# Efficient attention followed by an MLP with exact GELU: order of the VectorE work between two chunks, kv scaled by ScalarE, v cast later

## The chip, the cores and the metric

The kernel runs on one core of a Trainium2 chip. The metric is the device time of one execution in microseconds (us). PE is the matrix engine, PEld its weight loads, DVE is VectorE, ACT is ScalarE, POOL is GpSimd, and SP issues most of the DMAs.

## The reference

```
B, H, S, D = 8, 8, 576, 64
q_s = exp(q) / sum over D            # softmax of each row of q
k_s = exp(k) / sum over S            # softmax of k along the sequence
kv  = einsum('bhsd,bhse->bhde', k_s, v)
att = einsum('bhsd,bhde->bhse', q_s, kv)
x   = att.transpose(0, 2, 1, 3).reshape(4608, 512)
h   = x @ w_in                       # 512 -> 2048
g   = 0.5 * h * (1 + erf(h / sqrt(2)))
out = g @ w_out                      # 2048 -> 512, fp32
```

(The reference subtracts the maximum before each exponential and adds 1e-09 to each sum.)

## The kernel before, in words

**Tiling.** The 4608 rows are worked in nine chunks c = 0 to 8. Chunk c < 8 is the first 512 rows of batch c; chunk 8 gathers the last 64 rows of the eight batches. All matrix work is in bf16 with fp32 sums in PSUM, whose eight banks of 128 x 512 fp32 are handed out by role names (`bb`, `ba`, `x0` to `x3`, `kv0`, `kv1`), and `turn_roles` permutes the roles after every chunk's hidden layer.

**Two phases per chunk.** From chunk 2 on, a chunk is `h_waves(c)`, the hidden layer with its GELU, and then `y_phase(c, ...)` (for chunk 8 `y_last`), the output layer. Both multiply 2 x 2 blocks with seven products in place of eight (Winograd's form of Strassen's scheme): PE issues seven products, and DVE and ACT form sums and differences before and after them.

In `h_waves` the products are `mm(m, q...)` for m = 1 to 7 and four column groups q. Each group has an accumulator of kind A (product 1, later 6, 7 and 4), one of kind B (5, later 3) and one of kind C (a `seed` copy of A, later 2). Products 5, 6, 7 and 4 read `t1`, `t2`, `t3`, `t4`, four differences of blocks of the transposed chunk `xT`, which `x_sums(c, (i,))` makes on DVE into the tile `quad_t` (512 columns of bf16 each). The start of `h_waves` for c > 2 is, in program order: `mm(1, 0, 1)`, `seed(0)` (ACT), `mm(5, 0, 1)`, `seed(1)` (ACT), two `p5_copy` (ACT, B into the SBUF tile `r`), `mm(6, 0, 1)`, `x_sums(c, (3,))`, `e_sum(0)` and `e_sum(1)` (DVE: A + r into B), `x_sums(c, (4,))`, `mm(2, 0, 1)`, GELU of C, `mm(7, 0, 1)`, and so on. `mm(7, q)` writes the accumulator that `e_sum(q)` reads, and so comes after it.

In `y_phase` for c > 2 the output block is built in two SBUF tiles `y_sb` of four parts c11, c12, c21, c22. Product 3 of the outer scheme is itself done by seven small products (class `Two`, results in the banks called `yf` and `yd`), which `t3.add` adds to c12 on DVE in pieces: "a", "b" and "c" come from `yd`, "e" and "d" from `yf`. The bank of `yd` has the role `kv1`, the bank of `yf` has the role `bb`. Product 4, `mm(4, pa, False)`, writes the bank `pa` after the DVE addition `tt(c22, halves(pa), c22)` has read it; ACT then copies `pa` to c21.

**Work for later chunks.** Between the small products and `mm(4)`, `next_x(c, nb, fn)` runs with nb = c + 2. It issues the matmuls of the next chunk's x (`x_all`) and copies them out of PSUM as `xT` (three copies by ACT, the second by DVE). It also issues the DMA transpose of q for chunk nb (`xbar_step`) and, while nb < 8, the kv product of batch nb (`kv_mm`, into the roles `kv0` and `kv1`) with its normalisation `kv_norm` on DVE. `x_sums(c + 1, (1,))` and `(2,)` stand around the additions "e" and "d" (argument `fn`) and `kv_norm`. For c = 6 and 7 there is no kv product.

POOL scales the exponentials of q for chunk nb (`q_scale_parts`, eight instructions), makes sums for `Two`, and casts v of batch nb to bf16 (`cast_v_all`, four instructions of line 190). The order on every engine is the order of the program.

Of the kernel before, what the change touches and what calls it, by code (L numbers as in the profile page):

```python
# [16 lines left out]
def kernel(  # L17
# [11 lines left out]
    nc = tc.nc  # L29
# [221 lines left out]
    def kv_step(b, mid=None):  # L251
# [3 lines left out]
            mid()  # L255
        kv_norm(b)

    def q_sums(b, i=0, n=1):

        w = H // n  # L260
        qsum = small.tile([128, J, w], FP32, tag="qsum")
        st[b]["recq"] = small.tile([128, J, w], FP32, tag="recq", name="recq")
        nc.vector.reduce_sum(out=qsum, in_=st[b]["eq"][:, :, i * w:(i + 1) * w, :], axis=AX.X)  # L263
        nc.vector.reciprocal(st[b]["recq"], qsum)  # L264
# [164 lines left out]
    def tt(out, in0, in1, op=ALU.add, eng=nc.vector):  # L429
        eng.tensor_tensor(out=out, in0=in0, in1=in1, op=op)  # L430
# [27 lines left out]
    def turn_roles():  # L458

        r = dict(roles)  # L460
        roles.update(bb=r["x3"], ba=r["kv1"], x0=r["bb"], x1=r["kv0"], x2=r["x0"], x3=r["ba"],
                     kv0=r["x1"], kv1=r["x2"])

    def h_waves(c, mid):


        h_begin(c)
        g, xT = st[c]["g"], st[c]["xT"]
        t1, t2, t3, t4 = (quad["t"][:, i] for i in range(4))
        mov = {1: xT[:, 0:2, 0:HT], 2: xT[:, 2:4, 0:HT], 3: xT[:, 2:4, HT:M], 4: t4, 5: t1, 6: t2, 7: t3}  # L470
        plain_w = {1: (0, 0), 2: (2, 0), 4: (2, HK)}
        sum_w = {3: 3, 5: 0, 6: 1, 7: 2}
        lo, hi = slice(0, HT), slice(HT, M)
        bank_of = {
            "A": ("x0", "bb", "x3", "ba"), "B": ("kv0", "kv1", "x1", "x2"), "C": ("x1", "x2", "kv0", "kv1"),
        }
        if mid:
            bank_of.update(B=("kv0", "kv1") * 2, C=("x1", "x2") * 2)
        held = {}

        def take(kind, q):
            held[kind, q] = bank(roles[bank_of[kind][q]], "q" + kind.lower(), (128, 2, HT))

        def mm(m, *qs):
            for q in qs:
                kind = {5: "B", 3: "B", 2: "C"}.get(m, "A")
                if m in (1, 5):
                    take(kind, q)
                for u in range(2):
                    for k in range(2):  # L490
                        if m in plain_w:
                            k0, t0 = plain_w[m]
                            t = 2 * q + t0 + u
                            w = wi_bf[:, k0 + k, t * 128:(t + 1) * 128]
                        else:
                            t = 2 * (q % 2) + u
                            w = quad["s"][q // 2][:, sum_w[m], k, t * 128:(t + 1) * 128]
                        nc.tensor.matmul(  # L498
                            held[kind, q][:, u], w, mov[m][:, k],
                            start=(m in (1, 5) and u == 0 and k == 0), stop=(k == 1),  # L500
                            skip_group_check=True,
                        )

        def seed(q, eng=nc.scalar.copy):
            take("C", q)
            eng(out=held["C", q], in_=held["A", q])

        def p5_copy(q, eng):
            held["r", q] = quad["r"][:, q]
            eng(out=held["r", q], in_=held["B", q])  # L510

        def e_sum(q):
            tt(held["B", q], held["A", q], held["r", q])

        def r_sum(q):
            tt(held["r", q], held["A", q], held["r", q])

        def gelu(kind, *qs):
            up, half = {"C": (1, lo), "B": (1, hi), "A": (0, lo), "r": (0, hi)}[kind]
            for q in qs:  # L520
                t = 2 * q + (0 if up else HK)
                nc.scalar.activation(out=g[:, t:t + 2, half], in_=held[kind, q], func=AF.Gelu)  # L522

        vcopy, scopy = nc.vector.tensor_copy, nc.scalar.copy
        mm(1, 0, 1)
        seed(0)
        if mid:
            seed(1)
            mm(1, 2, 3)
            mm(2, 0, 1)  # L530
            gelu("C", 0, 1)
            mm(5, 0, 1)
            p5_copy(0, scopy)
            p5_copy(1, scopy)
            x_sums(c, (3, 4))
            seed(2, vcopy)
            seed(3, vcopy)
            mm(6, 0, 1)
            e_sum(0)
            e_sum(1)  # L540
            mid()
            mm(2, 2, 3)
            gelu("C", 2, 3)
            mm(7, 0, 1)
            r_sum(0)
            r_sum(1)
            mm(3, 0, 1)
            gelu("B", 0, 1)
            mm(6, 2)
            mm(5, 2, 3)  # L550
            p5_copy(2, scopy)
            p5_copy(3, scopy)
            mm(6, 3)
            e_sum(2)
            e_sum(3)
            gelu("r", 0, 1)
            mm(4, 0, 1)
            gelu("A", 0, 1)
            mm(7, 2, 3)
            r_sum(2)  # L560
            r_sum(3)
            s_parts(c, 0, 4, (1,))
            gelu("r", 2, 3)
            mm(3, 2, 3)
            mm(4, 2, 3)
        else:
            mm(5, 0, 1)
            seed(1)
            p5_copy(0, scopy)
            p5_copy(1, scopy)  # L570
            mm(6, 0, 1)
            x_sums(c, (3,))
            e_sum(0)
            e_sum(1)
            x_sums(c, (4,))
            mm(2, 0, 1)
            gelu("C", 0, 1)
            mm(7, 0, 1)
            r_sum(0)
            r_sum(1)  # L580
            mm(3, 0, 1)
            for q in (2, 3):
                mm(5, q)
                mm(1, q)
            mm(4, 0, 1)
            gelu("r", 0)
            gelu("B", 0, 1)
            gelu("r", 1)
            seed(2)
            seed(3)  # L590
            gelu("A", 0, 1)
            p5_copy(2, vcopy)
            p5_copy(3, vcopy)
            s_parts(c, 0, 4, (1,))
            mm(6, 2, 3)
            e_sum(2)
            e_sum(3)
            s_parts(c, 0, 4, (2,))
            mm(2, 2, 3)
            gelu("C", 2, 3)  # L600
            mm(7, 2, 3)
            r_sum(2)
            r_sum(3)
            gelu("r", 2, 3)
            mm(3, 2, 3)
            mm(4, 2, 3)
        gelu("B", 2, 3)
        gelu("A", 2, 3)
        if mid:
            s_parts(c, 0, 4, (2, 3))  # L610
            s_parts(c, 4, 4, (1,))
            s_parts(c, 0, 4, (4,))
            s_parts(c, 4, 4, (2, 3, 4))
        else:
            s_parts(c, 0, 4, (3, 4))
            s_parts(c, 4, 4, (1, 2, 3, 4))
        turn_roles()
        if mid:
            roles.update(ba=roles["x2"], x2=roles["ba"])
# [133 lines left out]
    def y_phase(c, ins):  # L753
# [8 lines left out]
        def halves(ps):  # L762
            return ps.rearrange("p (j n) -> p j n", j=2)
# [34 lines left out]
        if t3:  # L798
            t3.mm(6, 5, 2, 4, 3)
            t3.add("b", c12)  # L800
            t3.mm(7)
            t3.add("c", c12)
        tt(c22, halves(pa), c22)
        after(7)
        if not t3:
            mm(3, pb, False)
# [337 lines left out]

        nc.gpsimd.tensor_copy(out=scr[:, 2:3], in_=s12[:, HK - 1, HT:HT + 1])

    def next_x(c, nb, fn=lambda: None):
        x_all(c + 1, [roles[n] for n in ("x0", "x1", "x2", "x3")], "svsv" if c == 2 else "svss")
        if nb <= B:
            xbar_step(nb)  # L1150

        def first():
            x_sums(c + 1, (1,))
            fn()

        if nb < B:
            kv_tiles(nb, (roles["kv0"], roles["kv1"]))
            kv_step(nb, first)
        else:
            first()  # L1160
        x_sums(c + 1, (2,))

    for c in range(2, B + 1):
        nb = c + 2
        if 2 < c < B - 2:
            cast_v_all(nb)
        h_waves(c, q_late if c == 2 else None)
        yi = {}
        if nb <= B:
            yi[1] = [lambda: exp_q(nb)]  # L1170
            yi[6] = [lambda: q_sums(nb), lambda: q_scale_parts(nb)]
            yi[7] = [lambda: table(AF.Gelu)]
        if nb + 1 < B:
            yi[6].append(lambda: load(nb + 1))
        elif nb + 1 == B:
            yi[6].append(load_qrest)
        if nb < B:
            yi[5] = [lambda: exp_k(nb), touch_s]
            if c == 2:
                yi[5].append(lambda: cast_v_all(nb))  # L1180
        if 2 < c < B:
            yi.setdefault(5, []).append(lambda: two[3].sums(c))
        if c < B:
            yi[3] = [lambda *fn: next_x(c, nb, *fn)]
            y_phase(c, yi)
        else:
            y_last(c)
# [30 lines left out]
```

## Time and profile before

| what | value |
|---|---|
| median of 3 runs | 258.31 us (257.98 to 258.41) |
| the profiled execution | 258.36 us, of which the span from the first to the last instruction is 256.5 us |
| granted TensorE clock | 1.00 |
| PE, PEld busy | 247.9 us (97%), 195.7 us (76%) |
| DVE, ACT, POOL busy | 198.7, 189.5, 82.1 us |
| PE's share of the chain that ended last | 87% |
| DVE's share of it | 6% |

Times in the trace count from the first instruction. A line of the timeline gives the start, the length from the first start to the last end of the merged instructions, the engine, the line of the kernel, the operation, output <- inputs, the shape and the count, and in brackets the idle time before it with what ended it. Instructions on one engine overlap a little at their ends, so the distance between two starts is shorter than the length of one.

### The profile page before, as it was taken

Reading aid. Unit: us, or ns where it says so; the run is one execution under the profiler, and the core shown is the slowest. Engines: PE = TensorE matmul, PEld = TensorE weight load, DVE = VectorE, ACT = ScalarE, POOL = GpSimd, SP = SyncE. Lnnn points to the kernel's source line nnn. Section 1 sums busy time; section 2 is a strip of 40 time slices with the busy share of each in tenths; the row PEclk is TensorE's granted clock in tenths of the full one; section 3 lists DMA queues with packets and bytes.
Section 4 is the critical chain, followed back from the end, with each engine's and each line's share of the span. In section 5 each row is a group of like instructions: output and inputs, shape, how many; then the busy total and the mean of one; then the engine's idle time right before and its main releaser. Section 6 shows DMA issues by size and latency. Waiting matters only on the chain.

```text
span 256.5 us, 6691 instructions
## 1 busy us (share of the span) xinstructions
PE 247.9 (97%) x2738; PEld 195.7 (76%) x2738; DVE 198.7 (77%) x358; ACT 189.5 (74%) x322; POOL 82.1 (32%) x109
## 2 busy tenths in 40 slices
PE   7799999999999999999999999999999899999994
PEld 3344444448888888888788978898889788988883
DVE  1878699878986977897989798987898689468932
ACT  4785988699887986898689868896886687068810
POOL 1530023001945078008900890086007600700000
PEclk9999999999999999999999999999999999999999
DMA  7999999993379998970389029201600160021033
GB/s 237 396 389 422 404 406 400 398 413 146 72 253 379 223 387 265 321 284 0 85 286 394 19 63 284 67 1 42 209 1 3 31 217 0 3 93 73 1 80 86
DMA packets 43166, 50.23 MB, mean 196 GB/s; under 512 B 20224, under 2 KB 30464, under 8 KB 42880
## 3 DMA queue, kind: packets, MB, share of 16 engines
q1 hardware_dynamic: 42416, 49.13, 55.8%
q10 hardware_dynamic: 720, 0.69, 1.1%
q8 instruction: 21, 0.34, 0.5%
q14 instruction: 9, 0.07, 0.1%
HBM read 36.70 MB, written 9.44 MB: 180 GB/s over the span
## 4 chain that ended last, share of the span: by engine, by line
PE 87%; DVE 6%; DMA 4%; issue 1%; ACT 0%; ACTq 0%; POOL 0%; DVEq 0%
PE qa L498 19%; PE ya L768 17%; PE ps L387 11%; PE qb L498 9%; PE yb L768 6%; PE ps L641 5%; PE qc L498 5%; PE yc L768 5%; DVE y_sb L430 3%; PE ya L837 2%; DMA f<-in_v_dram 2%; DMA touch<-in_moe_w_in_dram 2%; PE yf L726 2%; DVE quad_t L430 2%; PE yb L837 1%; PE yd L726 1%
## 5 line engine op out<-in xcount | busy, mean ns | idle before, releaser
L768 PEld LDWEIGHTS <-g 128*128 128x128 bf16 x448 | 43.1, 98 | 6.8 <-issue 1.4
L498 PEld LDWEIGHTS <-quad_s 128*128 128x128 bf16 x448 | 43.4, 98 | 6.2 <-DVE quad_t L430 0.9
L498 PEld LDWEIGHTS <-wi_bf 128*128 128x128 bf16 x336 | 32.9, 98 | 4.7 <-issue 0.8
L498 PE MATMUL qa<-quad_t,quad_s 128*128 128x256 bf16 x224 | 29.2, 273 | 0.3 <-DVE quad_t L430 0.2
L387 PE MATMUL ps<-xT,wi_bf 128*128 128x512 bf16 x128 | 28.1, 379 | 0.0
L768 PE MATMUL ya<-w,g 128*128 128x256 bf16 x224 | 26.8, 273 | 1.0 <-DVE y_sb L430 1.0
L768 PEld LDWEIGHTS <-s 128*128 128x128 bf16 x256 | 25.0, 98 | 2.9
L430 DVE TENSOR_TENSOR qb<-qa,r 128x512 f32<-128x512 f32 x28 | 18.2, 694 | 9.7 <-PE qa L498 5.1
L278 POOL TENSOR_TENSOR e<-e,recq 128x256 bf16<-128x256 bf16 x40 | 24.0, 637 | 4.6 <-issue 2.7
L269 POOL TENSOR_TENSOR e<-e,recq 128x1024 bf16<-128x1024 bf16 (+1 forms) x4 | 9.3, 2332 | 48.5 <-DVE recq L264 41.8
L380 ACT CAST xT<-ps 128x512 bf16<-128x512 f32 x23 | 12.3, 593 | 16.7 <-PE ps L358 8.4
L263 DVE TENSOR_REDUCE qsum<-e 128x16 f32<-128x1024 bf16 (+1 forms) x12 | 20.9, 1742 | 4.8 <-ACT e L173 4.8
L387 PEld LDWEIGHTS <-wi_bf 128*128 128x128 bf16 x128 | 12.4, 98 | 15.2 <-issue 0.5
L393 ACT ACTIVATE g<-ps 128x512 bf16<-128x512 f32 x32 | 17.6, 602 | 6.1 <-PE ps L387 5.8
L173 ACT ACTIVATE e<-f 128x512 bf16<-128x512 f32 (+1 forms) x42 | 20.5, 556 | 1.9 <-DMA f<-in_q_dram 1.7
L522 ACT ACTIVATE g<-r 128x512 bf16<-128x512 f32 x28 | 17.3, 631 | 5.8 <-DVE r L430 5.8
L430 POOL TENSOR_TENSOR two<-s 128x512 bf16<-128x512 bf16 x10 | 11.6, 1157 | 31.1 <-DVE s L430 31.1
L522 ACT ACTIVATE g<-qc 128x512 bf16<-128x512 f32 x28 | 15.3, 594 | 8.4 <-PE qc L498 8.3
L190 POOL CAST v_aug<-f 128x576 bf16<-128x576 f32 x25 | 18.0, 756 | 4.1 <-DMA f<-in_v_dram 3.1
L430 DVE TENSOR_TENSOR r<-qa,r 128x512 f32<-128x512 f32 x28 | 18.0, 684 | 1.0 <-PE qa L498 0.7
L178 ACT ACTIVATE ek<-f 128x2304 bf16<-128x2304 f32 (+1 forms) x10 | 17.3, 1728 | 0.6 <-DMA f<-in_k_dram 0.5
L768 PE MATMUL yb<-wo_bf,s 128*128 128x256 bf16 x144 | 17.2, 273 | 0.0
(111 smaller groups left out, 493.4 us busy)
## 6 DMA issues: line engine op xcount, KB each, us to landing
out_dram<-y_sb SPq DMA_DIRECT2D x16, 512.0 KB, 4.0
f<-in_k_dram SPq DMA_DIRECT2D x6, 1152.0 KB, 10.1
f<-in_v_dram SPq DMA_DIRECT2D x6, 1152.0 KB, 11.7
f<-in_q_dram SPq DMA_DIRECT2D x6, 1024.0 KB, 7.6
w<-in_moe_w_in_dram SPq DMA_DIRECT2D x6, 512.0 KB, 8.7
f<-in_v_dram SPq DMA_DIRECT2D x8, 288.0 KB, 6.4
f<-in_q_dram SPq DMA_DIRECT2D x4, 512.0 KB, 9.0
w<-in_moe_w_out_dram SPq DMA_DIRECT2D x2, 1024.0 KB, 11.6
```

Source lines behind the costliest of these rows:

```text
L173: nc.scalar.activation(out=dst[:, i], in_=src[:, u], func=AF.Exp)
L178: nc.scalar.activation(out=ek[b % 2][:, i:i + n], in_=st[b]["kf"][:, i:i + n].rearrange("p x (n d) -> p x n d", n=NS), func=AF.Exp,)
L190: eng.tensor_copy(out=o, in_=i)
L263: nc.vector.reduce_sum(out=qsum, in_=st[b]["eq"][:, :, i * w:(i + 1) * w, :], axis=AX.X)
L278: nc.gpsimd.tensor_tensor(out=e, in0=e, op=ALU.mult, in1=st[b]["recq"][:, j, i:i + 4].unsqueeze(2).to_broadcast([128, 4, D]),)
L387: nc.tensor.matmul(ps, wi_bf[:, dm, t * 128:(t + 1) * 128], st[c]["xT"][:, dm, :], start=(dm == 0), stop=(dm == NDM - 1),)
L393: nc.scalar.activation(out=st[c]["g"][:, t, :], in_=ps, func=AF.Gelu)
L430: eng.tensor_tensor(out=out, in0=in0, in1=in1, op=op)
L498: nc.tensor.matmul(held[kind, q][:, u], w, mov[m][:, k], start=(m in (1, 5) and u == 0 and k == 0), stop=(k == 1), skip_group_check=True,)
L522: nc.scalar.activation(out=g[:, t:t + 2, half], in_=held[kind, q], func=AF.Gelu)
L641: nc.tensor.matmul(ps, st[c]["g"][:, t, j * 128:(j + 1) * 128], wo_bf[:, t, :], start=(t == 0), stop=(t == NDF - 1),)
L768: nc.tensor.matmul(ps[:, j * HN:(j + 1) * HN], act[m][:, k, j * 128:(j + 1) * 128], wgt[m][:, k, :], start=(first and k == 0 and j == 0), ...
```

## The change

From chunk 3 on (the variant of `next_x` that is called with `fn`):

- Both DVE differences `t1` and `t2` come ahead of the additions "e" and "d"; these come behind `t2`.
- kv is normalised by the new `kv_scale`: DVE makes the two reciprocals, and ACT multiplies by them in four copies of 64 columns whose scale is read from SBUF, in place of two DVE multiplications.
- For c = 6 and 7 the addition "c" comes behind the one that reads `pa`.
- `cast_v_all` for chunks 3 to 5 moves from ahead of `h_waves` to behind `x_sums(c, (4,))`, with a small POOL copy that reads `t4` ahead of it.
- The second accumulator of kind A takes the bank with the role `x3`, and the third the one with `bb` (before the other way round); `turn_roles` is changed to match.

```diff
+    def kv_scale(b):
+        recs = []
+        for ps in st[b]["kvall"]:
+            rec = small.tile([128, 2], FP32, tag="reck")
+            nc.vector.reciprocal(rec, ps[:, :, D])
+            recs.append(rec)
+        for i, ps in enumerate(st[b]["kvall"]):
+            for u in range(2):
+                nc.scalar.activation(
+                    out=kvc[b][:, 2 * i + u], in_=ps[:, u, 0:D], func=AF.Copy, scale=recs[i][:, u:u + 1],
+                )
...
     def turn_roles():
-        roles.update(bb=r["x3"], ba=r["kv1"], x0=r["bb"], x1=r["kv0"], x2=r["x0"], x3=r["ba"],
+        roles.update(bb=r["bb"], ba=r["kv1"], x0=r["x3"], x1=r["kv0"], x2=r["x0"], x3=r["ba"],
                      kv0=r["x1"], kv1=r["x2"])
...
-            "A": ("x0", "bb", "x3", "ba"), "B": ("kv0", "kv1", "x1", "x2"), "C": ("x1", "x2", "kv0", "kv1"),
+            "A": ("x0", "x3", "bb", "ba"), "B": ("kv0", "kv1", "x1", "x2"), "C": ("x1", "x2", "kv0", "kv1"),
...
             x_sums(c, (4,))
+            if c + 2 < B:
+                nc.gpsimd.tensor_copy(out=scr[:, 2:3], in_=t4[:, 0, 0:1])
+                cast_v_all(c + 2)
             mm(2, 0, 1)
...
             t3.mm(7)
+            if c + 2 < B:
+                t3.add("c", c12)
+        tt(c22, halves(pa), c22)
+        if t3 and c + 2 >= B:
             t3.add("c", c12)
-        tt(c22, halves(pa), c22)
         after(7)
...
-    def next_x(c, nb, fn=lambda: None):
-        x_all(c + 1, [roles[n] for n in ("x0", "x1", "x2", "x3")], "svsv" if c == 2 else "svss")
+    def next_x(c, nb, fn=None):
+        x_all(c + 1, [roles[n] for n in ("x0", "x1", "x2", "x3")], "svss" if fn else "svsv")
         if nb <= B:
             xbar_step(nb)
-
-        def first():
-            x_sums(c + 1, (1,))
-            fn()
-
         if nb < B:
             kv_tiles(nb, (roles["kv0"], roles["kv1"]))
-            kv_step(nb, first)
+            if fn:
+                kv_mm(nb, 0)
+                kv_mm(nb, 1)
+                x_sums(c + 1, (1,))
+                kv_scale(nb)
+            else:
+                kv_step(nb, lambda: x_sums(c + 1, (1,)))
         else:
-            first()
+            x_sums(c + 1, (1,))
         x_sums(c + 1, (2,))
+        if fn:
+            fn()

     for c in range(2, B + 1):
         nb = c + 2
-        if 2 < c < B - 2:
-            cast_v_all(nb)
         h_waves(c, q_late if c == 2 else None)
```

## The prediction

> **What bounds the kernel now.** I read the page's busy times first, then the chain that ended last. PE is busy for 97% of the span and carries 87% of that chain. DVE carries 6%, so there are places where PE waits for DVE. The chain in order of time shows where: it leaves PE at 121.60, 147.73, 199.66 and 225.47 us, each time between the small products of one chunk and the hidden layer of the next. I call these places 3/4, 4/5, 6/7 and 7/8 after the chunks they join. Next I cut the span into phases with the table of windows (window, its length, busy us and count of PE, PEld, DVE, ACT, POOL, the clock, the DMA share, GB/s).
>
> ```profile
> 99.04:111.27 12.23, 12.23 (x114) 10.96 (x113) 9.33 (x17) 10.15 (x20) 2.50 (x4) 1.00 0.97 300
> 124.72:137.40 12.68, 12.53 (x115) 10.79 (x113) 11.37 (x23) 10.19 (x20) 3.29 (x5) 1.00 0.86 272
> 150.82:163.52 12.70, 12.55 (x115) 10.78 (x113) 11.38 (x23) 10.22 (x20) 3.32 (x5) 1.00 0.79 208
> 176.94:189.33 12.39, 12.39 (x115) 10.87 (x113) 10.48 (x23) 10.34 (x20) 0.51 (x1) 1.00 0.41 129
> 202.60:215.13 12.53, 12.43 (x115) 11.00 (x113) 9.96 (x19) 10.22 (x20) 0.66 (x2) 1.00 0.40 127
> 228.45:240.68 12.23, 12.23 (x114) 10.96 (x113) 9.48 (x18) 10.15 (x20) 0.00 (x0) 1.00 0.23 88
> ```
>
> These are the hidden layers of chunks 3 to 8, the same PE work each. Chunks 3 and 8 take 12.23 us; the others lose 0.45, 0.47, 0.16 and 0.30. The output phases lose too where there is no kv product: in the timeline of PE the x matmuls of 6/7 start at 199.56 and eight take 0.46 (as 121.49 to 121.95), so `mm(4)` could follow at 200.02, but starts at 200.74. That is 0.72 lost. At 7/8 the 64 short x matmuls start at 225.36 and last about 0.56, and `mm(4)` starts at 226.54, 0.62 lost. All losses come to 2.72 us, the most that this change can give.
>
> The timelines show the cause. DVE at 3/4, with ACT's line 814 (copy c21), 506 (`seed`), 510 (`p5_copy`):
>
> ```profile
> 121.60 0.42 DVE L430 TENSOR_TENSOR y_sb<-y_sb,yd 128x256 f32<-128x256 f32 x1 [0.60 <-PE yd L726]
> 121.94 0.68 DVE L430 TENSOR_TENSOR y_sb<-ya,y_sb 128x512 f32<-128x512 f32 x1
> 122.54 0.68 DVE L378 CAST xT<-ps 128x512 bf16<-128x512 f32 x1
> 123.33 0.82 DVE L430 TENSOR_TENSOR quad_t<-xT 128x512 bf16<-128x512 bf16 x1
> 124.07 0.99 DVE L430 TENSOR_TENSOR y_sb<-y_sb,yf 128x512 f32<-128x512 f32 x2
> ...
> 125.79 0.90 DVE L430 TENSOR_TENSOR quad_t<-xT,quad_t 128x512 bf16<-128x512 bf16 x1
> 126.61 0.88 DVE L430 TENSOR_TENSOR quad_t<-xT 128x512 bf16<-128x512 bf16 x1
> 127.46 1.30 DVE L430 TENSOR_TENSOR qb<-qa,r 128x512 f32<-128x512 f32 x2
> ```
> ```profile
> 124.77 0.59 ACT L814 COPY y_sb<-ya 128x512 f32<-128x512 f32 x1 [1.26 <-PE ya L768]
> 125.26 1.12 ACT L506 COPY qc<-qa 128x512 f32<-128x512 f32 x2
> 126.29 1.08 ACT L510 COPY r<-qb 128x512 f32<-128x512 f32 x2
> ```
> ```profile
> 126.74 1.05 PE L498 MATMUL qa<-quad_t,quad_s 128*128 128x256 bf16 x8 [0.15 <-DVE quad_t L430]
> ```
>
> DVE runs without a gap from 121.60; `t2` (125.79) stands last in its queue and ends at 126.69, and `mm(6)` starts at 126.74, though PE could have had it at 124.57 + 2 x 0.87 = 126.31. The kv banks, free at 125.47, and "d", done at 125.07, cost `mm(5)` and `mm(1, 1)` the rest. At 6/7 the releaser is the addition that reads `pa`:
>
> ```profile
> 200.74 1.91 PE L768 MATMUL ya<-w,g 128*128 128x256 bf16 x16 [0.55 <-DVE y_sb L430]
> ```
> ```profile
> 199.66 0.42 DVE L430 TENSOR_TENSOR y_sb<-y_sb,yd 128x256 f32<-128x256 f32 x1 [0.60 <-PE yd L726]
> 200.00 0.68 DVE L430 TENSOR_TENSOR y_sb<-ya,y_sb 128x512 f32<-128x512 f32 x1
> ```
>
> The second of these needs only `mm(7)`, done by 198.3, but stands behind "c", which waits for the last small product.
>
> **The change part by part.** *"c" behind the `pa` addition (6/7 and 7/8).* At 6/7 that addition follows "b" at 199.06 and ends at 199.74, before the x matmuls do; `mm(4)` moves from 200.74 to 200.02. "c" takes 199.66 to 200.00, and the x copy starts when its matmuls are done, about 200.1, in place of 200.60, `t1` follows at 200.9 and `t2` at 201.7. `mm(1, 1)`, 0.27 late before because "e" and "d" ended at 203.12 in the bank it needs, now needs the bank of x3, which ACT leaves at 201.57, earlier than its turn at 202.2. Both losses go: 0.72 + 0.30 = 1.02. At 7/8 `mm(4)` moves by the 0.62; `t1` then ends near 227.0, ahead of `mm(5)` at 228.6.
>
> *`t2` early, "e" and "d" late (3/4 to 5/6).* DVE after `t1`: two reciprocals (0.19 each), `t2` at 124.45. POOL still scales q until 125.19, and `t1`, beside it, took 0.82 (0.42 at 97.56, where POOL worked too, and 0.43 at 227.19, where it did not); of the two I give `t2` the 0.82. It ends by 125.3 and `mm(6)` never waits. "e" and "d" (0.92) and `t3` follow and end by 126.7; the bank `bb` is next needed by `mm(1, 2)`, about 7 us after `mm(1, 0)`; the store of that block leaves 1.2 us later, and nothing waits for it.
>
> *kv on ACT.* DVE loses two multiplications of 0.21 distance; ACT gets four copies. They stand between the x copies (done 123.51) and c21. The first can start when the first reciprocal is done, 124.07 + 0.16 + 0.04 = 124.27. No row shows a copy with its scale in SBUF. From below: 128x256 takes 0.37 and 128x512 0.59, so 64 columns take 0.21, and ACT's distance in a row is 0.10 shorter than the length: 0.12. From above: the 128x256 copy, not overlapped, 0.37. A gain is excluded, since ACT had no such work. The rows say no more, so I take the middle, 0.24. By the Trainium skill ("ScalarE: Activation LUTs", What ACT_TABLE_LOAD costs), 186 ns + 0.833 per column, 93 more for a scale in SBUF and 93 of overlap give 0.24 as an estimate and so the same sum.
>
> Four make 0.96: c21 starts at 125.23, 0.46 late. Queued behind it are two seeds and two `p5_copy`, so the first `p5_copy` ends at 127.34 and releases `e_sum(0)` at 127.38, in place of 127.46 (DVE came last then). `e_sum(1)` ends at 128.67 and `mm(7, 1)` goes at 128.71 against 128.94: of the 0.45, 0.22 is gained, and ACT is what is late next. The same at 4/5 (first copy 150.40, c21 151.36 for 150.86): `e_sum(1)` ends at 154.84, `mm(7, 1)` at 154.88 for 155.07, 0.19 gained. At 5/6 the copies end at 177.49 where c21 started at 176.98; `e_sum(1)` then ends at 180.88 for 180.69, and `mm(7, 1)` goes at 180.92 for 180.87: 0.05 lost.
>
> *v cast later.* POOL casts from about 0.5 us after `t4` starts (103.0 at chunk 3 for 99.91), four in 2.5 to 2.9. Their first reader is the next kv product, 16 us on. SP issues the load of the following v when that buffer is free: 103.56 becomes about 105.7, ahead of its next entry at 125.22. Cost nothing; without that slack a late load would stop SP's stores. The gain, `t3` at 0.42 again, is under ACT's path. At 2/3 the casts began behind `t2`, nothing to gain.
>
> *Bank roles.* At chunk 2 `mm(1, 1)` now needs bank 5, copied out by DVE by 73.31; its turn is 73.49. Nothing.
>
> Sum: 0.22 + 0.19 - 0.05 + 1.02 + 0.62 = 2.00. The profiled execution took 258.36, 0.05 above the median; 256.36, told as 256.4.
>
> **Rivals.** *Cheap copies.* At 0.12 each c21 is on time within 0.1, `e_sum` no longer binds, and nearly all 2.72 comes: 255.7. For it: copies in a row overlap. Against: a scale must be read.
>
> *Dear but hidden in part.* At 0.37 each of the three places loses 0.52 more, 1.56: 257.9, no change that a measurement can tell (0.2%, 0.5 us).
>
> *The ACT queue takes back everything.* The place is the same queue: c21, seeds, `p5_copy`, `e_sum`, `mm(7, 1)`. The point of decision is 0.24 + 2.00 / 12 = 0.41 a copy. At 0.59, the price of a whole 128x512 copy, the three places lose 4.2 more: 260.6. The trace speaks against it: ACT's length falls with the columns. For it: each copy waits on a semaphore of DVE, and a fixed part, 0.16 in those rows, is most of its price. The Trainium skill (same page, Rules for kernel authors) gives multiplications to VectorE, not ScalarE; by that rule this case is the result, and the trace agrees so far as VectorE took only 0.42 for the two.
>
> *The last two places give nothing.* If `mm(4)` has another late input, the sum is 0.36: 258.0. Against: the trace names the DVE addition at both, and `g` and the weights are long ready.
>
> **How the numbers follow.** The forecast has 0.60, cheap copies 0.18, dear ones 0.07, nothing at the last two 0.05, the queue 0.10. Faster 0.81 (the first two and a little of the dear case), same 0.09, slower 0.10. The range takes cheap copies in at 255.6 and ends at the dear case, 257.9.
>
> **What would show it.** Right: `mm(4)` directly behind the x matmuls at 6/7 and 7/8; `mm(6)` with no wait for `quad_t`; hidden layers of chunks 7 and 8 at 12.23 and those of 4 and 5 at 12.4 to 12.5; `e_sum(0)` released by ACT's `r`; four ACT rows of 128x64 at a distance of 0.24. Wrong: a table load beside these rows, a distance above 0.41, or a new wait of `mm(1)` for the bank of x3.

## The result and the profile after

The changed kernel takes 255.84 us (median of 4 runs, 255.67 to 256.00) against 258.27 (median of 4, 257.98 to 258.41): a ratio of 0.9907, 95% interval 0.9890 to 0.9924. The profiled execution took 255.67 us with a span of 253.9.

First the hidden layers of chunks 4 to 8 in the table of windows, in the columns of the prediction. They lasted 12.68, 12.70, 12.39, 12.53 and 12.23 us before.

```profile
124.31:136.58 12.27, 12.27 (x115) 10.96 (x113) 10.04 (x19) 10.51 (x23) 3.27 (x6) 1.00 0.88 274
149.98:162.31 12.33, 12.33 (x115) 10.98 (x113) 10.09 (x19) 10.57 (x23) 3.33 (x6) 1.00 0.81 214
175.71:188.04 12.33, 12.33 (x115) 11.00 (x113) 10.09 (x19) 10.57 (x23) 0.70 (x1) 1.00 0.41 130
200.72:212.93 12.21, 12.21 (x115) 10.94 (x113) 10.36 (x19) 10.11 (x20) 1.42 (x3) 1.00 0.41 130
225.76:237.99 12.23, 12.23 (x115) 10.96 (x113) 9.88 (x18) 10.13 (x20) 0.00 (x0) 1.00 0.22 88
```

Then the timeline of VectorE at 3/4, to be held against that of the prediction:

```profile
122.91 0.82 DVE L444 TENSOR_TENSOR quad_t<-xT 128x512 bf16<-128x512 bf16 x1
123.66 0.22 DVE L264 RECIPROCAL rec<-kv 128x2 f32<-128x2 f32 x2
123.84 0.65 DVE L444 TENSOR_TENSOR quad_t<-xT,quad_t 128x512 bf16<-128x512 bf16 x1
124.42 0.99 DVE L444 TENSOR_TENSOR y_sb<-y_sb,yf 128x512 f32<-128x512 f32 x2
125.33 0.42 DVE L444 TENSOR_TENSOR quad_t<-xT 128x512 bf16<-128x512 bf16 x1
126.78 1.30 DVE L444 TENSOR_TENSOR qb<-qa,r 128x512 f32<-128x512 f32 x2 [1.03 <-ACT r L524]
```

`t2` (the third line) ends at 124.49, and `mm(6)` is due at 125.91: 1.4 us to spare where it was 0.38 late. VectorE, which had no gap before, now idles 1.03 us ahead of `e_sum`, and the bracket names what it waits for, ACT's `p5_copy`. ACT's timeline at the same place, with line 268 (the scaled copies), 834 (c21), 520 (`seed`) and 524 (`p5_copy`):

```profile
123.85 0.93 ACT L268 ACTIVATE kvc<-kv,rec 128x64 bf16<-128x64 f32 x4 [0.76 <-DVE rec L264]
124.66 0.60 ACT L834 COPY y_sb<-ya 128x512 f32<-128x512 f32 x1
125.12 1.10 ACT L520 COPY qc<-qa 128x512 f32<-128x512 f32 x2
126.11 1.12 ACT L524 COPY r<-qb 128x512 f32<-128x512 f32 x2
```

The bracket shows that ACT idles 0.76 us until the reciprocal is there (it idled 1.26 ahead of c21 before). The four copies then take 0.81 up to the start of c21. Part of that falls into time in which ACT was idle, and the rest pushes c21 back: it starts 0.50 behind `mm(1, 0)` (124.16), before 0.20 behind it (124.77 and 124.57). At 6/7 PE's timeline shows `mm(4)` with no bracket, 0.56 us behind the start of the x matmuls, where it was 1.18:

```profile
198.26 0.63 PE L367 MATMUL ps<-qT,kvc 64*64 64x512 bf16 x8
198.82 1.92 PE L785 MATMUL ya<-w,g 128*128 128x256 bf16 x16
```

The page's chain carries the sum of this: VectorE's share, 6% before, is gone.

```profile
PE 93%; DMA 4%; ACT 0%; ACTq 0%; issue 0%; DVE 0%; POOL 0%
```

### The profile page after: what moved, and what is told of

Same layout as the page of the kernel before. It is cut to its first block, busy times and chain, and to the rows that moved or that the text cites. A ratio compares the mean times of both kernels' runs of the same rounds, so it can differ in the third digit from the quotient of the medians.

```text
span 253.9 us, 6709 instructions
## 1 busy us (share of the span) xinstructions
PE 247.0 (97%) x2738; PEld 195.9 (77%) x2738; DVE 195.9 (77%) x352; ACT 191.4 (75%) x334; POOL 82.6 (33%) x112
## 4 chain that ended last, share of the span: by engine, by line
PE 93%; DMA 4%; ACT 0%; ACTq 0%; issue 0%; DVE 0%; POOL 0%
PE ya L785 20%; PE qa L512 19%; PE ps L401 11%; PE qb L512 10%; PE yb L785 6%; PE ps L658 6%; PE qc L512 5%; PE yc L785 5%; PE ya L857 2%; DMA touch<-in_moe_w_in_dram 2%; DMA f<-in_v_dram 2%; PE kv L225 2%; PE yf L743 2%; PE ps L367 2%; PE yb L857 1%; PE yd L743 1%
## 5 line engine op out<-in xcount | busy, mean ns | idle before, releaser
L292 POOL TENSOR_TENSOR e<-e,recq 128x256 bf16<-128x256 bf16 x40 | 24.7, 655 | 4.0 <-issue 2.1
L401 PEld LDWEIGHTS <-wi_bf 128*128 128x128 bf16 x128 | 12.4, 98 | 15.1 <-issue 0.5
L190 POOL CAST v_aug<-f 128x576 bf16<-128x576 f32 x25 | 17.3, 732 | 2.7 <-DMA f<-in_v_dram 2.6
```

Source lines behind the costliest of these rows:

```text
L190: eng.tensor_copy(out=o, in_=i)
L292: nc.gpsimd.tensor_tensor(out=e, in0=e, op=ALU.mult, in1=st[b]["recq"][:, j, i:i + 4].unsqueeze(2).to_broadcast([128, 4, D]),)
L401: nc.tensor.matmul(ps, wi_bf[:, dm, t * 128:(t + 1) * 128], st[c]["xT"][:, dm, :], start=(dm == 0), stop=(dm == NDM - 1),)
```

## The experiments

All of them are compared below by one number for each chunk: the time from the first `mm(1)` of a chunk's hidden layer to the next chunk's, in PE's timeline. The distance from chunk 4 to 5 holds what is lost at 3/4, that from 5 to 6 what is lost at 4/5. That from 6 to 7 holds the loss of chunk 6's hidden layer (5/6) and the late `mm(4)` at 6/7; that from 7 to 8 the late `mm(1, 1)` of 6/7 and the late `mm(4)` at 7/8. The distance from 3 to 4 is 25.69 or 25.70 in every kernel, so the table leaves it out. The last two columns are the ratio to the kernel before with its interval, and the median. Each kernel was timed beside runs of the kernel before, whose median lay between 258.13 and 258.34 from one occasion to the next, so rows from different occasions are better held together by their ratios and distances than by their medians.

| kernel | 4 to 5 | 5 to 6 | 6 to 7 | 7 to 8 | ratio | us |
|---|---|---|---|---|---|---|
| before | 26.09 | 26.12 | 25.70 | 25.81 | | 258.27 |
| changed | 25.68 | 25.73 | 25.00 | 25.05 | 0.9907 (0.9890 to 0.9924) | 255.84 |
| e1, kv on VectorE | 25.65 | 25.65 | 24.93 | 25.05 | 0.9909 (0.9894 to 0.9924) | 255.74 |
| e2, c first | 25.69 | 25.73 | 25.63 | 25.54 | 0.9954 (0.9942 to 0.9967) | 257.02 |
| e3, banks as before | 26.51 | 26.57 | 25.84 | 26.09 | 1.0077 (1.0064 to 1.0090) | 260.18 |
| e4, casts early | 25.69 | 25.73 | 25.02 | 25.04 | 0.9913 (0.9899 to 0.9926) | 256.00 |
| e5, c alone | 26.09 | 26.13 | 25.09 | 25.35 | 0.9958 (0.9946 to 0.9971) | 257.01 |
| e6, e and d early | 26.60 | 26.65 | 25.93 | 25.04 | 1.0017 (1.0008 to 1.0026) | 258.63 |
| e7, copies twice | 26.51 | 26.55 | 25.83 | 25.04 | 1.0014 (1.0005 to 1.0023) | 258.42 |
| e8, kv and casts as before | 25.65 | 25.65 | 24.94 | 25.04 | 0.9909 (0.9894 to 0.9924) | 255.71 |
| e9, c and late casts | 25.76 | 25.80 | 25.09 | 25.34 | 0.9926 (0.9912 to 0.9940) | 256.43 |
| e10, c and banks | 26.08 | 26.12 | 25.08 | 25.04 | 0.9943 (0.9930 to 0.9955) | 256.93 |

### One part undone

**e1: kv by VectorE, at the place of the copies.**

```diff
-                kv_scale(nb)
+                kv_norm(nb)
```

> The changed kernel with kv normalised by VectorE again (two reciprocals and two multiplications, at the place of the new copies: between t1 and t2). Theory: in the changed kernel ACT's queue is what ends last at 3/4, 4/5 and 5/6 (e_sum(0) is released by the first p5_copy), and t2 has time: with 0.42 us of multiplications ahead of it, it ends by 125.4, before mm(6) is due at 125.91. So nothing is lost, and the 0.17 us that the hidden layers of chunks 4, 5 and 6 still lose go too: 255.7 us, e_sum released by PE or DVE's own queue. Rival (the multiplications on VectorE were what made t2 late): mm(6) waits again, 0.3 us at each of the three places, 256.7 us.

Measured 255.74 us. The theory holds. VectorE's timeline has `t2` end at 125.27, with `mm(6)` due at 126.12 in this run, and PE releases `e_sum`:

```profile
124.67 0.60 DVE L444 TENSOR_TENSOR quad_t<-xT,quad_t 128x512 bf16<-128x512 bf16 x1
125.20 1.00 DVE L444 TENSOR_TENSOR y_sb<-y_sb,yf 128x512 f32<-128x512 f32 x2
126.11 0.42 DVE L444 TENSOR_TENSOR quad_t<-xT 128x512 bf16<-128x512 bf16 x1
126.83 1.30 DVE L444 TENSOR_TENSOR qb<-qa,r 128x512 f32<-128x512 f32 x2 [0.29 <-PE qa L512]
```

The distances are 0.03, 0.08 and 0.07 shorter than in the changed kernel, 0.18 in all against the expected 0.17. The times of the two kernels do not tell them apart. Moving kv to ACT brought nothing to this kernel.

**e2: "c" first again.**

```diff
-            if c + 2 < B:
-                t3.add("c", c12)
-        tt(c22, halves(pa), c22)
-        if t3 and c + 2 >= B:
-            t3.add("c", c12)
+            t3.add("c", c12)
+        tt(c22, halves(pa), c22)
```

> The changed kernel with the addition c ahead of the one that reads pa at 6/7 and 7/8 again. Theory: mm(4) waits for the VectorE addition again, 0.62 us at 6/7 and 0.51 us at 7/8, so 1.13 us slower than the changed kernel: 257.0 us, the other places as they are. Rival (the order of t2, e and d is what helped there): under 0.3 us lost, 256.1 us.

Measured 257.02, with 0.63 and 0.49 lost in the two columns in question. PE's timeline shows the old releaser again:

```profile
199.83 1.91 PE L785 MATMUL ya<-w,g 128*128 128x256 bf16 x16 [0.56 <-DVE y_sb L444]
```

**e3: the banks as before.**

```diff
-        roles.update(bb=r["bb"], ba=r["kv1"], x0=r["x3"], ...
+        roles.update(bb=r["x3"], ba=r["kv1"], x0=r["bb"], ...
...
-            "A": ("x0", "x3", "bb", "ba"), ...
+            "A": ("x0", "bb", "x3", "ba"), ...
```

> The changed kernel with the two banks as before: the second accumulator of kind A takes the bank that e and d read. Theory: e and d now stand behind t2 and so mm(1, 1) waits for them: 0.87, 0.87, 0.91, 1.07 and 0.63 us at the five places, less the 0.17 us of waits that they swallow: 4.2 us slower than the changed kernel, 260.0 us, and slower than the kernel before. Rival (the banks matter little, the late additions are covered): 256 us.

Measured 260.18, slower than the kernel before. `mm(1, 1)`, 0.44 behind `mm(1, 0)` elsewhere, comes 1.30 behind it, released by the late additions; five such places are in the waits of PE:

```profile
124.71 0.60 PE L512 MATMUL qa<-xT,wi_bf 128*128 128x256 bf16 x4
126.01 0.60 PE L512 MATMUL qa<-xT,wi_bf 128*128 128x256 bf16 x4 [0.70 <-DVE y_sb L444]
```
```profile
PE qa L512 <- DVE y_sb L444: 3.6, 5, 0.9
```

(The wait at 7/8 falls into chunk 8 and so lies behind the table's last column.) The exchange of two bank roles is what allows "e" and "d" to stand late.

**e4: the casts early.**

```diff
             x_sums(c, (4,))
-            if c + 2 < B:
-                nc.gpsimd.tensor_copy(out=scr[:, 2:3], in_=t4[:, 0, 0:1])
-                cast_v_all(c + 2)
...
         nb = c + 2
+        if 2 < c < B - 2:
+            cast_v_all(nb)
         h_waves(c, ...
```

> The changed kernel with the casts of v ahead of the hidden layer again, so that GpSimd casts as soon as it has scaled q. Theory: the casts at 3/4 and 4/5 run beside t3, which takes 0.88 in place of 0.42 us and ends at 126.2, before e_sum(0) at 126.8: no loss, 255.8 us. Rival (the casts beside the differences were part of the loss): 0.4 us at each of the two places, 256.6 us.

Measured 256.00, and distances as in the changed kernel within 0.02. `t3` beside the casts took 0.52, not the 0.88 expected. In the changed kernel the later casts are worth nothing.

### ACT's queue

**e6: "e" and "d" ahead of the reciprocals.**

```diff
                 x_sums(c + 1, (1,))
+                if fn:
+                    fn()
                 kv_scale(nb)
...
-        if fn:
-            fn()
```

(and for c = 6 and 7 `fn()` directly behind `x_sums(c + 1, (1,))`.)

> The changed kernel with e and d directly behind t1 again, ahead of the reciprocals and of t2; kv still on ACT. Theory (ACT's queue): t2 is still in time (ends by 125.7, mm(6) is due at 125.91), but the reciprocals come 0.91 us later and with them the four copies, c21, the seeds and the p5_copy; e_sum(0) starts 0.9 us later and mm(7, 1) with it: 0.8 to 0.9 us at each of 3/4, 4/5 and 5/6, 258.4 us, with no wait of mm(6) for quad_t. Rival (t2's time alone matters): under 0.1 us at each place, 256.0 us.

Measured 258.63, 0.92 or 0.93 more in each of the three columns with kv. `mm(6)` does not wait for `t2`, which ends at 125.23. The lines of VectorE, of PE, and of PE's waits:

```profile
124.83 0.40 DVE L444 TENSOR_TENSOR quad_t<-xT,quad_t 128x512 bf16<-128x512 bf16 x1
```
```profile
125.46 1.03 PE L512 MATMUL qb<-quad_t,quad_s 128*128 128x256 bf16 x8
126.83 1.08 PE L512 MATMUL qa<-quad_t,quad_s 128*128 128x256 bf16 x8 [0.34 <-ACT qc L520]
```
```profile
PE qb L512 <- ACT kvc L268: 0.4, 2, 0.2
```

What PE does wait for had been missing from the theory, and there are two such waits. `mm(5)`, the first of the lines of PE, writes the kv banks, which the copies now leave later: due at 125.14 (124.27 + 0.87), it starts at 125.46, 0.32 late. Then `mm(6, 0)` adds into the accumulator that `seed(0)` reads, and the seeds stand behind the copies in ACT's queue: due at 126.02, it starts at 126.83, so another 0.49 is lost. Both stop PE before `e_sum` does.

**e7: each copy twice.**

```diff
-            for u in range(2):
+            for u in (0, 1, 0, 1):
```

> The changed kernel with each of the four scaled copies done twice, so that ACT spends 0.81 us more on them at 3/4, 4/5 and 5/6. Theory (the queue from the copies to mm(7, 1) has no slack left): 0.81 us lost at each, 2.4 us, 258.2 us, no different from the kernel before, since eight copies at 0.20 us are worth four at 0.40, next to the 0.41 at which the prediction put the break-even. Rival (ACT has slack, as its idle time of 0.25 us before the first GELU says): at most 1.6 us, 257.4 us.

Measured 258.42, between 0.82 and 0.83 more in each of the three columns: what was put into ACT's queue there came out whole at the end. Eight copies lasted 1.75 us, four 0.93: 0.205 apart. PE again waits for the seed, and `mm(5)` ahead of it lasts 1.22 in place of 1.04, which fits its second half waiting for the second kv bank (the last copy ends at 125.90, that half is due at 125.77):

```profile
125.33 1.22 PE L512 MATMUL qb<-quad_t,quad_s 128*128 128x256 bf16 x8
126.91 1.08 PE L512 MATMUL qa<-quad_t,quad_s 128*128 128x256 bf16 x8 [0.37 <-ACT qc L520]
```

### The parts alone

**e5: "c" behind the `pa` addition, and nothing else of the change.** The edit is that of e2 the other way round, made to the kernel before.

> The kernel before with one part of the change alone: for c = 6 and 7 the addition c behind the one that reads pa. Theory: mm(4) moves up by 0.62 us at 6/7 and 0.51 us at 7/8; at 6/7 mm(1, 1) still waits for e and d in its bank, 0.35 us in place of 0.27: 1.05 us faster than before, 257.1 us. Rival (without the other parts the differences then stop PE in place of mm(4), and the gain is given back): 257.9 us or more.

Measured 257.01: 0.61 and 0.46 gained in the last two distances, nothing elsewhere.

**e9: e5 and the late casts.** The edit is that of e4 the other way round.

> The kernel before with c behind the addition that reads pa, and with the casts of v behind t4; kv, e, d and the banks as before. Theory: without the casts beside it t2 takes 0.42 in place of 0.90 us at 3/4 and 4/5, ends at about 126.2 on the clock of the kernel before and no longer stops mm(6), due at 126.31; what is left there are the short waits for the bank of e and d and for the kv banks, as at 5/6 (0.16 us in all): 0.6 us faster than with c alone, 256.4 us. Rival (the casts cost nothing, as their removal from the changed kernel showed): 257.0 us.

Measured 256.43; 0.33 less than e5 in each of the first two distances, 0.66 in all. `t2`, last in VectorE's queue as it was in the kernel before, and 0.90 long there beside the casts, is now 0.41 long and in time:

```profile
125.42 0.41 DVE L430 TENSOR_TENSOR quad_t<-xT,quad_t 128x512 bf16<-128x512 bf16 x1
```
```profile
126.06 1.04 PE L498 MATMUL qa<-quad_t,quad_s 128*128 128x256 bf16 x8
```

The same part that brings nothing in the changed kernel (e4) wins back most of the loss at 3/4 and 4/5 when "e", "d" and kv stay where they were.

**e10: e5 and the new bank roles.** The edit is that of e3 the other way round.

> The kernel before with c behind the addition that reads pa, and with the new bank roles; e and d directly behind t1, kv on VectorE and the casts early as before. Theory: mm(1, 1) no longer waits for e and d (0.3 us at 6/7, 0.15 at 5/6), but at 3/4 and 4/5 mm(6) still waits for t2, which takes over what mm(1, 1) gives up: 0.45 us faster than with c alone, 256.6 us; with e and d behind t2 as well it is the kernel of 255.71 us, so that move is worth the last 0.85. Rival (the banks alone do it, without the new order): 255.8 us.

Measured 256.93, so less than the expected gain. Only the last distance is shorter than in e5, by 0.31: `mm(1, 1)` at 6/7. The 0.15 expected at 5/6 did not come. There `mm(1)` gained it, but `mm(5)`, due at 177.65, started at 177.79, since the first kv bank was free only at 177.73 (177.44 + 0.29):

```profile
177.44 0.29 DVE L246 TENSOR_TENSOR kvc<-kv,rec 128x128 bf16<-128x128 f32 x1
```

**e8: the changed kernel with kv on VectorE and early casts,** the edits of e1 and e4 together. What is left is three parts: "c" late, the banks, and "e" and "d" behind `t2`.

> The changed kernel with kv normalised by VectorE and the casts early, both as before: what is left of the change is the bank roles, e and d behind t2, and c behind the addition that reads pa. Theory: t2 ends by 125.3 and t3, beside the casts, near 127.1, so e_sum(1) ends by 128.5, when mm(7, 1) is due: at most 0.2 us lost, 255.7 to 256.0 us, so these two parts bring nothing here. Rival (one of the two is needed for the gain, either being enough): e_sum late by 0.4 us at each of 3/4 and 4/5, 256.6 us.

Measured 255.71, with distances as short as those of e1, 0.18 less in sum than the changed kernel; as for e1 the times do not separate the two. Beside e10 it has 0.43, 0.47 and 0.14 less in the first three distances. That is the worth of standing "e" and "d" behind kv and `t2`, once the banks allow it.

## Why the prediction was right, and where its sizes were off

The forecast of 256.4 lies 0.56 above the measured median, within its range, and the mechanisms were those named. The distances of the table sum to 103.72 before and 101.46 after, a gain of 2.26 against the 2.00 of the sum. The two profiled executions differ by more, 2.69: 0.41 lies ahead of chunk 3, whose hidden layer starts at 98.88 and 98.47; over all kernels that start varies between 98.47 and 99.01, and it lies at 98.61 in e5, whose program is that of the kernel before up to chunk 6. So the 0.41 is not shown to belong to the change. The sum came nearer than its terms, and that is luck: the two `mm(4)` were 0.21 too high together, the three places with kv 0.48 too low.

- **"c" behind the `pa` addition and the bank of `mm(1, 1)`**, 1.02 at 6/7 and 0.62 at 7/8. The mechanism is shown by e2, e5 and e10. The two `mm(4)` were each sized about 0.1 too high: I let `mm(4)` follow the x matmuls at 0.46 and 0.56, but it follows at 0.56 and 0.67. The losses at hand were thus 2.51, not 2.72. Measured: 0.62 and 0.51 for the two `mm(4)`, and 0.31 for `mm(1, 1)`.
- **`t2` early.** Right that `mm(6)` never waits; `t2` took 0.65, not 0.82, which costs nothing.
- **kv on ACT**, the term furthest off: 0.22, 0.19 and -0.05 forecast at 3/4, 4/5 and 5/6; the hidden layers gained 0.41, 0.37 and 0.06. Those of chunks 4 and 5 took 12.27 and 12.33, not the 12.4 to 12.5 named as a sign. The price of a copy was too high: 0.205 apart, for the 0.24 taken between 0.12 and 0.37, so four make 0.82, and c21 is 0.30 late in place of 0.46. The Trainium skill ("ScalarE: Activation LUTs", What ACT_TABLE_LOAD costs) gives, as an estimate, 0.332 for one copy and 0.24 for the distance; the trace has 0.314 and 0.205. What is late next was right: `e_sum` is released by ACT's `r`.
- **What I did not see** is that the kv copies were not needed at all. I weighed each part against the kernel before, one by one, where `t2` is 0.38 late; any one of "e" and "d" behind it or the casts out of its way makes up for most of that (e8, e9). With "e" and "d" behind `t2`, neither the casts (e4) nor the kv copies (e1) have anything left to gain.
- **The rival of ACT's queue.** Its point of decision, 0.41 a copy, was tried at 0.41 (e7): 258.42, 0.14% (0.05 to 0.23) above the kernel before. The queue is as tight as the rival said, only the price was low. What it stops first is `mm(5)` behind the kv banks and `mm(6)` behind the seed (e6, e7), not `mm(7)` behind `e_sum`.
- **Casts later** at no cost, and the load of v that follows at none, as forecast. **Bank roles** at chunk 2: nothing, as forecast; but the exchange is no detail, since without it the whole change turns into a loss (e3).

A rule of the Trainium skill bears on the casts ("SBUF — State Buffer", Who interferes with whom): a VectorE instruction with two inputs in SBUF contends with a GpSimd instruction that reads SBUF. The trace agrees in the case that mattered, 0.90 against 0.41 for the same `t2` with and without the casts beside it. So does 0.65 for `t2` in the changed kernel, wholly beside the scaling of q (to 124.97), against 0.40 in e6, where the scaling ended at 124.89, 0.06 after `t2` began. The traces also show that the price varies: in the kernel before, `t1` took 0.42 at 97.56 and 0.82 at 123.33, both beside the scaling; beside the casts, `t3` took 0.88 there and 0.52 in e4. No run here isolates why. GpSimd's lines for the scaling, in the changed kernel and in e6:

```profile
119.99 4.98 POOL L292 TENSOR_TENSOR e<-e,recq 128x256 bf16<-128x256 bf16 x8 [0.22 <-issue]
```
```profile
120.10 4.79 POOL L292 TENSOR_TENSOR e<-e,recq 128x256 bf16<-128x256 bf16 x8 [0.25 <-issue]
```

## What to carry to other kernels

When an engine's queue delays a busy one, list what stands in front of the late instruction and what each entry's own reader could bear. Here reordering three entries ("c", "e" and "d") and exchanging two buffers' roles gave all of the gain (e8). The work moved to another engine gave none: once `t2` was in time VectorE had nothing left to be relieved of (e1), and the other engine's queue led to the same matmuls (e6, e7). Price parts of a change together as well as one by one: two parts that each remove most of the same 0.4 us are worth 0.4, not 0.8, and a part that looks like bookkeeping (a bank role) can be the one that the others need.

## What the runs showed of the hardware

- A ScalarE copy of 128x64 from PSUM with its scale in SBUF took 0.314 us (median of 12), and 0.205 from one to the next (e7 against the changed kernel).
- Where a matmul with a 128*128 tile follows those with 64*64 tiles or the other way round, PE's timeline has about 0.1 us more between them: eight 64x512 x matmuls are followed by `mm(4)` at 0.56 us, and by the 64*64 kv matmuls at 0.46 (121.08 to 121.54). The small products ahead of them, groups of four matmuls 0.22 apart, are followed by the x matmuls at 0.31 (120.77 to 121.08). It is the same before and after. It was not tried by itself, so that the change of tile is the cause is not shown.
